# The last A12 x B21 products as seven products of halves, with sums made by accumulating transfers

## The chip, the core and the metric

The kernel runs on one core of a Trainium2 chip. The metric is device time of one execution in microseconds; the figure given for the kernel before is a median of three runs. The core's engines are TensorE (PE, matrix products; PEld is its weight load), VectorE (DVE), ScalarE (ACT), GpSimd (POOL) and SyncE (SP). SP issues most loads, POOL most stores and every transfer that adds into its destination. PSUM is where products are summed, here as four pairs of banks of 128 x 2 x 512 fp32; SBUF holds everything else that is worked on; DRAM holds inputs, outputs and scratch.

## What is computed

With x of 2048 tokens by 512, the output is a gated mix of a Fourier mixing and a SwiGLU layer:

```python
g = sigmoid((x * gate_w).sum(-1))
a = x @ dft_hid_re.T;  b = x @ dft_hid_im.T
y = dft_seq_re @ a - dft_seq_im @ b
h = silu(x @ w1) * (x @ w3)
out = g * y + (1 - g) * (h @ w2)
```

The hidden width F is 1376, padded to eleven chunks of 128. All of it is fp32.

## The kernel before, in words

**Three matmuls per product.** Every fp32 operand is split into a high part (fp32r, a rounded copy made by ScalarE) and a low part (the rest, by VectorE); `split` does it in lines 62 to 64. `mm3` (lines 69 to 72) then issues three matmuls for a pair of operands: high by high, high by low, low by high.

**Seven products instead of eight.** Each large product is cut in two halves in every direction, and the Strassen-Winograd scheme makes seven products of the halves. They are named P1 to P7. P1 = A11 x B11, P5, P6, P3, P7 and P4 use sums of blocks, and P2 = A12 x B21. P1, P6, P7 and P4 are summed one after another in one pair of PSUM banks, P5 and P3 in a second, P2 in a third. After each product the state of its banks is taken out where the scheme needs it.

**Stages.** The first stage makes a and b (scratch `ab`). The second makes the SwiGLU hidden values (scratch `hsp`); between its products, hooks call `work`, which takes the tasks of the list `later` one by one: these form the A-side operands of the last stage by `forms` (line 327) and store them, split, in the scratch `fsp`. The last stage is what the change touches. It has six *blocks*, (m, j): m = 0 is h @ w2, m = 1 the real part, m = 2 the imaginary part; j is the group of 1024 tokens. Blocks 4 and 5 are m = 2 with j = 0 and 1. In a block of m = 1 or 2 the A side is 512 output features by 2048 tokens to be summed over, the B side 2048 by 1024 tokens out (from the input `cc`).

**Steps.** A product of a block runs as four steps q of the list `STEPS` (lines 382 to 390), in the order of `CHAIN`: P1, P5, P6, P3, P7, P2, P4. A step of blocks 1 to 5 at full width is 12 matmuls of 512 columns. `step` (line 562) issues the matmuls of a step, then calls `advance`, then the tasks booked for that step in `TASKS`, and after a product's last step takes out the banks and calls `finish`, which makes the output of that quarter (for m = 2 with loaded tiles of the earlier blocks, `load_other`) and stores it.

**What runs ahead.** `advance(n)` does three things for later steps: `load_c(n + 8)` loads raw B blocks (B11, B12, B22, B21; a list sorted by the step that needs them less a small lead), `sum_c(n + 4)` makes the sums F1 = B11 + B12, F2 = F1 + B22, F3 = B12 + B22 and F4 = F2 + B21 in place by VectorE, and `split_c(n + 3)` splits the step's B operand. `BY_DMA` (line 413) names block 2: there F3 is made by a transfer of GpSimd that adds B12 from DRAM into the tile of B22, after B22's split (line 455).

**Buffers.** The pool f4 has 19 buffers of 128 x 1024 fp32 and holds raw B tiles, gates, sums taken from PSUM and tiles for outputs. zo has 8 (the split B operands of four steps). op has 28 and holds the split A operands: 7 products x 4 steps, loaded by `load_a` from `fsp`. The tile framework places the semaphore waits and picks buffers; it may also put an engine's instructions in another order than they are written, except that the loads issued through `fetch` keep theirs.

**The end.** The split sources of the last two steps (P4 of block 5) are multiplied by the gate first (lines 449 to 451), and these two steps write fresh banks in two row halves, so that the last output goes out in small pieces.

Of the kernel before, what the change touches and what calls it, by code (L numbers as in the profile page):

```python
# [7 lines left out]
F32 = mybir.dt.float32  # L8
# [4 lines left out]
P = 128  # L13
# [11 lines left out]
def fnet_swiglu_gate_kernel(  # L25
# [54 lines left out]
    ysp = dram.tile([G, 2, 2, P, 1024], F32, tag="ysp", name="ysp")  # L80
    PRODS = ("P1", "P5", "P6", "P3", "P7", "P2", "P4")
    wlsp = dram.tile([P, 1024], F32, tag="wlsp", name="wlsp")
    fsp = dram.tile([3, len(PRODS), NQ, P, 1024], F32, tag="fsp", name="fsp")


# [241 lines left out]
    def forms(m, q, ks, keep):  # L327
# [37 lines left out]

        return [load] + [lambda k=k: one(k) for k in ks]

    def fetch(o, i):
        tc.keep_in_program_order(nc.sync.dma_start(o, i))
# [9 lines left out]
    CHAIN = (("P1", "B11"), ("P5", "F1"), ("P6", "F2"), ("P3", "B22"),  # L379
             ("P7", "F3"), ("P2", "B21"), ("P4", "F4"))  # L380
    PLAIN = {"P3": "n1", "P7": "n1", "P2": "n0", "P4": "n01"}
    STEPS, AT = [], {}
    for b, (m, j) in enumerate(BLOCKS):
        for k, form in CHAIN:
            for q in range(NQS[m]):
                AT[b, k, q] = len(STEPS)
                STEPS.append((b, k, q, form))
            if m == 0 and k in PLAIN:
                STEPS.append((b, k, "pl", PLAIN[k]))
    NEED = (("B11", "P1", 0), ("B12", "P5", 1), ("B22", "P6", 1), ("B21", "P2", 0))  # L390
    LOADS = sorted((AT[b, k, q] - e, b, blk, q) for b, (m, j) in enumerate(BLOCKS)
                   for blk, k, e in NEED for q in range(NQS[m]))
    LEAD, AHEAD = 3, 5
    RAW, ZO, PL = {}, {}, {}

    def block(b, k, q):
        m, j = BLOCKS[b]
        if m == 0:
            v = hsp[j, int(k[1]) - 1, int(k[2]) - 1, 2 * q : min(2 * q + 2, NP)]
            return v.rearrange("c p n -> p c n")  # L400
        return half(cc[m - 1, j, ("B11", "B12", "B22", "B21").index(k), q])

    def chunks(b, q):
        return width(BLOCKS[b][0], q) // 256

    def load_c(n):
        while LOADS and LOADS[0][0] <= n:
            _, b, k, q = LOADS.pop(0)
            w = chunks(b, q)
            r = RAW[b, k, q] = raw(f"{k}_{b}_{q}", w * 512)  # L410
            fetch(half(r, w), block(b, k, q))

    BY_DMA = (2,)

    def sum_c(n):
        if not 0 <= n < len(STEPS):
            return
        b, k, q, form = STEPS[n]
        o = {"F1": "B12", "F2": "B22", "F4": "B21", "F3": "B22"}.get(form)
        if not o or q == "pl" or form == "F3" and b in BY_DMA:  # L420
            return
        t = RAW[b, "B12" if form == "F3" else "B11", q]
        nc.vector.tensor_add(t, t, RAW[b, o, q])  # L423

    def split_c(n):
        if not 0 <= n < len(STEPS):
            return
        b, k, q, form = STEPS[n]
        if q == "pl":
            r = PL[b]  # L430
            if form == "n1" and k == "P3":
                t = zo.tile([P, 1024], F32R, tag="zo", name=f"zp{n}")
                split(t[:, :512], t[:, 512:], r["n1"])
                r["z"] = t
            elif form == "n1":
                ZO[n] = r["z"][:, :512], r["z"][:, 512:]
                return
# [8 lines left out]
        f3 = "B22" if b in BY_DMA else "B12"  # L446
        src = RAW[b, {"F1": "B11", "F2": "B11", "F4": "B11", "F3": f3}.get(form, form), q]
        h, l = (zo.tile([P, w], F32R, tag="zo", name=f"z{v}{n}") for v in "hl")
        if n >= len(STEPS) - 2:

            nc.vector.tensor_mul(half(src), half(src), twice(GT[b], 0))
        split(h, l, src)
        ZO[n] = h, l
        if form == "B22" and b in BY_DMA:
            nc.gpsimd.dma_start(half(src, chunks(b, q)), block(b, "B12", q), accum_op=ALU.add)

    def advance(n):
        load_c(n + LEAD + AHEAD)
# [44 lines left out]
    def twice(t, n):  # L503
        return half(t)[:, n : n + 1].to_broadcast([P, 2, 512])
# [54 lines left out]
    U, BANKS, WHOLE = {}, {}, {}  # L559
    QUARTER = {"P3": (0, 1), "P7": (1, 1), "P2": (0, 0), "P4": (1, 0)}  # L560

    def step(n):
        b, k, q, form = STEPS[n]
        m, j = BLOCKS[b]
        end = b == len(BLOCKS) - 1
# [12 lines left out]
        fin = STEPS[n + 1][1] != k if n + 1 < len(STEPS) else True  # L578
# [24 lines left out]
        advance(n)  # L603
        for f in TASKS.pop(n, ()):
            f()
        if n == len(STEPS) - 3:
            U[k, b] = half(raw(f"u{k}_{b}"))
            finish(b, *QUARTER[k], U[k, b], whole)
        if not fin or n == len(STEPS) - 1:
            return  # L610
        if k in ("P1", "P5", "P6"):
            t = U[k, b] = half(raw(f"u{k}_{b}"))
            nc.scalar.activation(flat(t), flat(whole), AF.Copy)
# [51 lines left out]
    later += prep_w2l()  # L665
    for q in range(NQ):
        later += forms(2, q, PRODS, False)
    for q in range(NQ):
        later += forms(1, q, ("P1", "P5", "P6", "P3"), False)
    per = -(-len(later) // ((NC - 1) * 5))  # L670
# [122 lines left out]
```

## Time and profile before

| | us |
|---|---|
| median of 3 runs (708.13 to 708.25) | 708.18 |
| the profiled execution, as timed | 709.88 |
| its span in the profile | 708.1 |
| PE busy in the span | 702.6 |
| VectorE busy | 565.5 |
| ScalarE busy | 337.7 |
| GpSimd busy | 80.1 |

How to read the lines that follow. A group of instructions shows line, engine, operation, the tile written, an arrow and the tiles read, shapes and count, then busy us and mean ns of one, then the engine's idle time ahead of them and what ended it. A line of waits names who waited for whom, with the sum in us, the number of waits and the longest. A line of the timeline has start, length and instruction. A line of windows has the stretch, its length, then busy us and instruction count for PE, PEld, VectorE, ScalarE and GpSimd, and last the granted clock of TensorE, the busy share of the DMA engines and GB/s. A line of transfers has the issuing queue, the count, the size and the us from issue to landing. Because helpers record the splits, sums and loads, one source line stands for many tiles.

### The profile page before, as it was taken

The numbers are of one execution on the slowest core, as the hardware profiler recorded it, in microseconds if no ns is written. First come the engines' busy times: TensorE is split into PE (matmuls) and PEld (weight loads), VectorE is DVE, ScalarE is ACT, GpSimd is POOL, SyncE is SP. The second block draws the span as 40 slices with busy tenths as digits, with TensorE's granted clock in tenths as the row PEclk, the third lists the DMA queues.
The fourth block names the chain that finished last, engine by engine and source line by source line (L and its number), as shares of the span: only waits on it lengthen the run. The fifth ranks groups of instructions, "written<-read, shape, count | busy, mean of one in ns | idle before, by whom it ended". The sixth has DMA issues, their size and how long they took to land.

```text
span 708.1 us, 8582 instructions
## 1 busy us (share of the span) xinstructions
PE 702.6 (99%) x3081; PEld 578.9 (82%) x3081; DVE 565.5 (80%) x600; ACT 337.7 (48%) x380; POOL 80.1 (11%) x139
## 2 busy tenths in 40 slices
PE   9999999999999999999999999999999999999997
PEld 6888888888888888888888888888888888888886
DVE  6994358878988886859968997679488977999695
ACT  5744146655555454464453375444443444344431
POOL 0010103322323221100000001000000000000000
PEclk9999999999999999999999999999999999999999
DMA  8356439989999899889978869916889928971402
GB/s 302 116 190 224 179 118 343 310 302 323 377 370 390 303 356 377 295 331 402 342 271 299 287 251 261 319 41 238 303 313 341 371 98 279 336 244 64 149 31 89
DMA packets 55530, 186.43 MB, mean 263 GB/s; under 512 B 6012, under 2 KB 6268, under 8 KB 55488
## 3 DMA queue, kind: packets, MB, share of 16 engines
q1 hardware_dynamic: 36432, 117.59, 47.1%
q0 software_dynamic: 18768, 67.91, 25.5%
q8 instruction: 24, 0.39, 0.2%
q10 hardware_dynamic: 288, 0.39, 0.2%
q14 instruction: 18, 0.15, 0.1%
HBM read 119.54 MB, written 66.33 MB: 262 GB/s over the span
## 4 chain that ended last, share of the span: by engine, by line
PE 99%; DMA 1%; ACT 0%; DVE 0%; DVEq 0%; issue 0%
PE P L71 57%; PE X L71 17%; PE dP L71 10%; PE Z L71 8%; PE Y L71 4%; PE last L71 1%; PE dP L185 1%; DMA dB<-dd 1%; ACT dB21h L63 0%; DVE uP L556 0%; DVEq L789 0%
## 5 line engine op out<-in xcount | busy, mean ns | idle before, releaser
L63 ACT ACTIVATE zh<-B 128x1024 fp32r<-128x1024 f32 x154 | 157.2, 1023 | 216.9 <-PE P L71 192.5
L64 DVE TENSOR_TENSOR zl<-B,zh 128x1024 fp32r<-128x1024 f32 x154 | 180.0, 1173 | 58.6 <-ACT zh L63 53.1
L71 PE MATMUL P<-zh,a2P 128*128 128x512 f32 x432 | 133.1, 389 | 0.0
L423 DVE TENSOR_TENSOR B<-B,B 128x1024 f32<-128x1024 f32 (+1 forms) x84 | 97.1, 1168 | 0.4
L71 PEld LDWEIGHTS P<-zh,a2P 128*128 128x128 f32 x432 | 81.1, 188 | 16.9
L71 PE MATMUL P<-zh,a0P 128*128 128x512 f32 x280 | 87.5, 389 | 0.0
L71 PE MATMUL P<-zl,a2P 128*128 128x512 f32 x216 | 84.0, 389 | 0.0
L71 PE MATMUL P<-zh,a1P 128*128 128x512 f32 x256 | 79.1, 389 | 0.0
L71 PEld LDWEIGHTS P<-zh,a0P 128*128 128x128 f32 x280 | 52.5, 188 | 10.9
L71 PE MATMUL P<-zh,f1P 128*128 128x512 f32 x192 | 59.4, 389 | 0.0
L71 PEld LDWEIGHTS P<-zh,a1P 128*128 128x128 f32 x256 | 48.0, 188 | 9.9
L71 PE MATMUL P<-zl,a0P 128*128 128x512 f32 x140 | 54.5, 389 | 0.0
L71 PE MATMUL P<-zl,a1P 128*128 128x512 f32 x128 | 49.8, 389 | 0.0
L71 PEld LDWEIGHTS P<-zl,a2P 128*128 128x128 f32 x216 | 40.5, 188 | 8.4
L71 PEld LDWEIGHTS P<-zh,f1P 128*128 128x128 f32 x192 | 36.0, 188 | 7.5
L71 PE MATMUL P<-zl,f1P 128*128 128x512 f32 x96 | 37.3, 389 | 0.0
L71 PEld LDWEIGHTS P<-zl,a0P 128*128 128x128 f32 x140 | 26.3, 188 | 5.5
L71 PEld LDWEIGHTS P<-zl,a1P 128*128 128x128 f32 x128 | 24.0, 188 | 5.0
L618 DVE TENSOR_TENSOR uP<-uP,P 128x1024 f32<-128x1024 f32 x18 | 21.9, 1218 | 3.8 <-PE P L71 3.8
L271 DVE TENSOR_TENSOR s<-s,Y 128x1024 f32<-128x1024 f32 x11 | 13.4, 1215 | 11.6 <-PE Y L71 9.7
L293 DVE TENSOR_TENSOR u<-u,X 128x1024 f32<-128x1024 f32 x11 | 13.4, 1218 | 10.5 <-PE X L71 10.4
L71 PEld LDWEIGHTS P<-zl,f1P 128*128 128x128 f32 x96 | 18.0, 188 | 3.8
(1258 smaller groups left out, 1312.5 us busy)
## 6 DMA issues: line engine op xcount, KB each, us to landing
B<-cc SPq DMA_DIRECT2D x64, 512.0 KB, 5.3
fsp<-f2P POOLq DMA_DIRECT2D x28, 512.0 KB, 5.7
a2P<-fsp SPq DMA_DIRECT2D x28, 512.0 KB, 5.3
r<-ab SPq DMA_DIRECT2D x24, 512.0 KB, 5.8
hsp<-u POOLq DMA_DIRECT2D x20, 512.0 KB, 6.4
fsp<-f1P POOLq DMA_DIRECT2D x16, 512.0 KB, 6.5
B<-hsp SPq DMA_DIRECT2D x16, 512.0 KB, 10.1
a1P<-fsp SPq DMA_DIRECT2D x16, 512.0 KB, 6.8
```

Of the source, the lines that this page charges most:

```text
L63: nc.scalar.activation(hi, src, AF.Copy)
L64: nc.vector.tensor_sub(lo, src, hi.bitcast(F32))
L71: nc.tensor.matmul(ps, u, v, start=first and n == 0, stop=last and n == 2, skip_group_check=chain)
L185: nc.tensor.matmul(ps[i // 2][:, i % 2], u[:, 0, i * P : (i + 1) * P], v[:, 0], start=n == 0, stop=False, skip_group_check=True)
L271: nc.vector.tensor_add(S1[c], S1[c], flat(y))
L293: nc.vector.tensor_add(u4, u4, flat(x))
L423: nc.vector.tensor_add(t, t, RAW[b, o, q])
L618: nc.vector.tensor_add(flat(t), flat(t), flat(whole))
```

## The change

In blocks 4 and 5 the product P2 is no longer run per block. Since A12 of the imaginary part is the same for both token groups, A12 x [B21 of group 0, B21 of group 1] is one product of 256 x 1024 by 1024 x 1024, and it is cut in halves once more: seven inner products of 128 x 512 by 512 x 512, named LP1 to LP7. Each is two half steps of 6 matmuls; the 14 half steps are put between the steps of blocks 4 and 5 (`inner_step`), two of them after P6 of each block and the others mostly after every second step.

- *Order.* The two blocks run P1, P5, P6, P7, P3, P4 (`LORDER`), so P7 is now ahead of P3.
- *A side.* `inner_forms` loads A12 again in block 2, makes the inner sums, splits them and stores them in the scratch `lsp`; `load_inner` loads each eight steps ahead of its use. The four P2 operands of m = 2 are not formed in the second stage any more (`later[-2]`).
- *B side.* The inner blocks LB11, LB12, LB21, LB22 are the halves of B21 of both groups (two tiles each). Their sums LF1, LF2 and LF4 are made in the tile of LB11 by accumulating transfers after each split, LF3 in the tile of LB12.
- *F4 and F3.* F4 of blocks 4 and 5 is made by accumulating B21 into the tile of F2 after its split, in place of a load of B21 and a VectorE sum. F3 of block 5 is made in a fresh tile: B12 is loaded again and B22 accumulated. F3 of block 4 stays on VectorE.
- *Outputs.* `inner` takes each inner product from a PSUM bank of the fourth pair: two as negated copies by ScalarE, five as half-size additions or subtractions by VectorE, into the tile of P1's sum of block 4 or 5. The quarter (0, 0) of block 4 is finished after LP4, in block 5, that of block 5 after LP3. P1's bank of block 5 is added to a tile that is there already, by VectorE, where ScalarE copied it.
- *The gate* is multiplied into B11 of the last two steps as tasks at P3 of block 5.

```diff
+    def inner_forms():
+        st = {}
...
+        def load():
+            for h in range(2):
+                st[h] = raw(f"rl{h}")
+                for q in range(2):
+                    nc.sync.dma_start(
+                        st[h][:, q * 512 : (q + 1) * 512], ab[1, 1, 2 * h + q, :, 0].rearrange("p i e -> p (i e)"))
+
+        def one(k):
...
+            t = f4.tile([P, 2, 512], F32R, tag="f4", name=f"fl{k}")
+            split(quads(t[:, 0]), quads(t[:, 1]), src)
+            nc.gpsimd.dma_start(lsp[PRODS.index(k)], flat(t.bitcast(F32)))
+
+        return [load] + [lambda k=k: one(k) for k in ("P1", "P5", "P6", "P3", "P7", "P2", "P4")]
+
+    def load_inner(k):
+        t = A["L", k] = op.tile([P, 2, 4, P], F32R, tag="op", name=f"al{k}")
+        fetch(t.bitcast(F32).rearrange("p v c e -> p (v c e)"), lsp[PRODS.index(k)])
...
+    LB = (4, 5)
+    FORM = dict(CHAIN)
+    INNER = [(k, h) for k in ("P1", "P2", "P5", "P6", "P7", "P4", "P3") for h in range(2)]
...
+    LORDER = ("P1", "P5", "P6", "P7", "P3", "P4")
     for b, (m, j) in enumerate(BLOCKS):
-        for k, form in CHAIN:
+        for k, form in ((k, FORM[k]) for k in LORDER) if b in LB else CHAIN:
             for q in range(NQS[m]):
                 AT[b, k, q] = len(STEPS)
                 STEPS.append((b, k, q, form))
+                if b in LB and q % 2 and (b, k) not in ((LB[0], "P1"), (LB[0], "P5"), (LB[0], "P6"), (LB[1], "P6")):
+                    if len(todo) > 2:
+                        inner_step()
+            if b in LB and k == "P6":
+
+                for _ in range(2):
+                    inner_step()
...
     LOADS = sorted((AT[b, k, q] - e, b, blk, q) for b, (m, j) in enumerate(BLOCKS)
-                   for blk, k, e in NEED for q in range(NQS[m]))
+                   for blk, k, e in NEED if not (b in LB and blk == "B21") for q in range(NQS[m]))
+    LOADS += [(AT["L", k, h] - e, LB[1], "L" + blk, h) for blk, k, e in
+              (("B11", "P1", 0), ("B12", "P7", 4), ("B21", "P2", 0), ("B22", "P3", 3)) for h in range(2)]
+    LOADS += [(AT[LB[1], "P7", q] - 3, LB[1], "F3", q) for q in range(NQ)]
+    LOADS.sort()
...
             fetch(half(r, w), block(b, k, q))
+            if k in ("LB12", "F3"):
+                add_block(r, b, {"LB12": "LB22", "F3": "B22"}[k], q)
+
+    def add_block(t, b, k, q):
+        nc.gpsimd.dma_start(half(t, chunks(b, q)), block(b, k, q), accum_op=ALU.add)
...
-        if not o or q == "pl" or form == "F3" and b in BY_DMA:
+        if not o or q == "pl" or form == "F3" and b in BY_DMA + LB[1:] or form == "F4" and b in LB:
             return
...
-        if n >= len(STEPS) - 2:
-
-            nc.vector.tensor_mul(half(src), half(src), twice(GT[b], 0))
         split(h, l, src)
         ZO[n] = h, l
         if form == "B22" and b in BY_DMA:
-            nc.gpsimd.dma_start(half(src, chunks(b, q)), block(b, "B12", q), accum_op=ALU.add)
+            add_block(src, b, "B12", q)
+        elif form == "F2" and b in LB:
+            add_block(src, b, "B21", q)
+        elif form in ("LB11", "LF1", "LF2"):
+            add_block(src, b, {"LB11": "LB12", "LF1": "LB22", "LF2": "LB21"}[form], q)
...
+    INTO = {"P1": (0, 0), "P5": (1, 1), "P6": (0, 1), "P2": (0, 0), "P7": (1, 1), "P4": (1, 0), "P3": (0, 1)}
+    LPS = {}
+
+    def inner(n):
+        b, k, h, form = STEPS[n]
+        k = k[1:]
+        if h == 0:
+            if not LPS:
+                z = pair(3, "Lx")
+                LPS.update(P1=z[:, 0], P5=z[:, 1], P2=z[:, 1])
+        ps = LPS[{"P6": "P1", "P7": "P1", "P4": "P1", "P3": "P5"}.get(k, k)]
+        w = A["L", k]
+        zh, zl = ZO.pop(n)
+        for i in range(2):
+            c = slice(i * 512, (i + 1) * 512)
+            mm3(ps, w[:, 0, 2 * h + i], w[:, 1, 2 * h + i], zh[:, c], zl[:, c],
+                k in ("P1", "P5", "P2") and h == 0 and i == 0, h == 1 and i == 1, True)
+        advance(n)
+        for f in TASKS.pop(n, ()):
+            f()
+        if h == 1:
+            r, g = INTO[k]
+            if k == "P5":
+                U["P1", LB[1]] = half(raw("uL"))
+            t = U["P1", LB[g]]
+            if k in ("P5", "P6"):
+                nc.scalar.activation(t[:, r], ps, AF.Copy, scale=-1.0)
+            else:
+                (nc.vector.tensor_sub if g else nc.vector.tensor_add)(t[:, r], t[:, r], ps)
+            if k in ("P4", "P3"):
+                finish(LB[g], 0, 0, t)
...
-        if k in ("P1", "P5", "P6"):
+        if (k, b) in U:
+            nc.vector.tensor_add(flat(U[k, b]), flat(U[k, b]), flat(whole))
+        elif k in ("P1", "P5", "P6"):
...
         later += forms(2, q, PRODS, False)
+        later[-2] = lambda: None
...
-    for i, (k, q) in enumerate((k, q) for k, _ in CHAIN for q in range(NQ)):
+    for i, (k, q) in enumerate((k, q) for k in LORDER for q in range(NQ)):
         TASKS.setdefault(AT[3, "P1", 0] + 1 + 7 * i // 4, []).append(lambda k=k, q=q: load_a(2, k, q))
+    for i, f in enumerate(inner_forms()):
+        TASKS.setdefault(AT[2, "P1", 0] + 13 + 2 * i, []).append(f)
+    for k, h in INNER:
+        if not h:
+            TASKS.setdefault(AT["L", k, 0] - 8, []).append(lambda k=k: load_inner(k))
+    def gated(q):
+
+        t = half(RAW[LB[1], "B11", q])
+        tc.keep_in_program_order(nc.vector.tensor_mul(t, t, twice(GT[LB[1]], 0)))
+
+    for q in (2, 3):
+        TASKS.setdefault(AT[LB[1], "P3", q - 2], []).append(lambda q=q: gated(q))
```

More of the change, by code (lines that the diff above doesn't have):

```diff
@@ L82, in fnet_swiglu_gate_kernel @@
     wlsp = dram.tile([P, 1024], F32, tag="wlsp", name="wlsp")
+    lsp = dram.tile([len(PRODS), P, 1024], F32, tag="lsp", name="lsp")
     fsp = dram.tile([3, len(PRODS), NQ, P, 1024], F32, tag="fsp", name="fsp")
@@ L366, in forms, with cols, quads @@
         return [load] + [lambda k=k: one(k) for k in ks]
+    def inner_forms():
+        st = {}
+        def cols(t, v):
+            return t.rearrange("p (c h e) -> p c h e", c=4, h=2)[:, :, v]
+        def quads(ap):
+            return ap.rearrange("p (c e) -> p c e", c=4)
+        def load():
[5 more added lines that the diff above has]
+        def one(k):
+            a11, a21, a12, a22 = cols(st[0], 0), cols(st[0], 1), cols(st[1], 0), cols(st[1], 1)
+            if k in ("P5", "P3"):
+                st["m"] = raw(f"ml{k}")
+            lo, hi = quads(st["m"][:, :512]) if "m" in st else None, quads(st["m"][:, 512:]) if "m" in st else None
+            if k == "P5":
+                src = st["s5"] = lo
+                nc.vector.tensor_sub(src, a22, a21)
+            elif k == "P6":
+                src = st["s6"] = hi
+                minus_sum(src, st["s5"], a11)
+            elif k == "P3":
+                src = lo
+                minus_sum(src, a12, st["s6"])
+            elif k == "P7":
+                src = hi
+                nc.vector.tensor_sub(src, a11, a21)
+            else:
+                src = {"P1": a11, "P2": a12, "P4": a22}[k]
+            t = f4.tile([P, 2, 512], F32R, tag="f4", name=f"fl{k}")
[5 more added lines that the diff above has]
+        fetch(t.bitcast(F32).rearrange("p v c e -> p (v c e)"), lsp[PRODS.index(k)])
     def fetch(o, i):
@@ L387, in fnet_swiglu_gate_kernel @@
                 STEPS.append((b, k, q, form))
+                if b in LB and q % 2 and (b, k) not in ((LB[0], "P1"), (LB[0], "P5"), (LB[0], "P6"), (LB[1], "P6")):
[4 more added lines that the diff above has]
+                    inner_step()
             if m == 0 and k in PLAIN:
                 STEPS.append((b, k, "pl", PLAIN[k]))
+    assert not todo
+    FINAL = {}
+    for n, (b, k, q, form) in enumerate(STEPS):
+        FINAL[b, k] = n
     NEED = (("B11", "P1", 0), ("B12", "P5", 1), ("B22", "P6", 1), ("B21", "P2", 0))
     LOADS = sorted((AT[b, k, q] - e, b, blk, q) for b, (m, j) in enumerate(BLOCKS)
[L392 removed]
+                   for blk, k, e in NEED if not (b in LB and blk == "B21") for q in range(NQS[m]))
[3 more added lines that the diff above has]
+    LOADS.sort()
     LEAD, AHEAD = 3, 5
@@ L397, in block @@
         m, j = BLOCKS[b]
+        if k[0] == "L":
+            return half(cc[m - 1, int(k[3]) - 1, 3, 2 * (int(k[2]) - 1) + q])
         if m == 0:
@@ L400, in block @@
             return v.rearrange("c p n -> p c n")
-        return half(cc[m - 1, j, ("B11", "B12", "B22", "B21").index(k), q])
+        return half(cc[m - 1, j, ("B11", "B12", "B22", "B21").index("B12" if k == "F3" else k), q])
     def chunks(b, q):
@@ L445, in split_c @@
         w = chunks(b, q) * 512
-        f3 = "B22" if b in BY_DMA else "B12"
-        src = RAW[b, {"F1": "B11", "F2": "B11", "F4": "B11", "F3": f3}.get(form, form), q]
+        f3 = "B22" if b in BY_DMA else "F3" if b == LB[1] else "B12"
+        inner = form[0] == "L"
+        blk = form[1:] if inner else form
+        src = RAW[b, "L" * inner + {"F1": "B11", "F2": "B11", "F4": "B11", "F3": "B12" if inner else f3}.get(blk, blk), q]
         h, l = (zo.tile([P, w], F32R, tag="zo", name=f"z{v}{n}") for v in "hl")
-        if n >= len(STEPS) - 2:
-            nc.vector.tensor_mul(half(src), half(src), twice(GT[b], 0))
         split(h, l, src)
@@ L564, in step @@
         m, j = BLOCKS[b]
+        if k[0] == "L":
+            if q == 0 and k in ("LP4", "LP3"):
+                load_other(LB[k == "LP3"], 0, 0)
+            return inner(n)
         end = b == len(BLOCKS) - 1
@@ L577, in step @@
         own = k in ("P1", "P5", "P2")
-        fin = STEPS[n + 1][1] != k if n + 1 < len(STEPS) else True
+        fin = n == FINAL[b, k]
         zh, zl = ZO.pop(n)
```

7 lines of the change are left out of this document (added).

## The prediction

> **What bounds the kernel now.** I read the page's engine shares first, then the chain of waits in order of time, then the windows of the last four blocks (76.2 us each, counted back from the end of the last product).
>
> ```profile
> span 708.1 us, 8582 instructions
> PE 702.6 (99%) x3081; PEld 578.9 (82%) x3081; DVE 565.5 (80%) x600; ACT 337.7 (48%) x380; POOL 80.1 (11%) x139
> ...
> 293.61 405.28 PE P L71 x1788
> 698.89 5.45 PE last L71 x24
> ...
> 399.60:475.80 76.20, 76.20 (x338) 63.10 (x337) 62.95 (x62) 37.46 (x43) 5.66 (x8) 1.00 0.69 226
> 552.00:628.20 76.20, 76.20 (x338) 63.10 (x337) 65.88 (x58) 32.53 (x32) 2.71 (x4) 1.00 0.75 269
> 628.20:704.40 76.20, 76.13 (x336) 62.69 (x334) 64.90 (x58) 29.09 (x28) 2.87 (x4) 1.00 0.30 102
> ```
>
> TensorE (PE) is the bound without a gap: the chain is matmul from 293.61 to 704.34, 405.28/1788 = 0.2267 us each, at granted clock 1.00. A step of 12 is 2.72 us, a half step of 6 is 1.36 us. So matmuls that go are time won, as long as nothing else makes PE wait. In the windows the last two columns are the share of the DMA engines and GB/s: VectorE (DVE) is at 86% in block 4 (552 to 628), the transfers at 0.75 there and 0.30 in block 5.
>
> What feeds PE is a split three steps ahead (ScalarE copy, VectorE subtract), and what feeds the split is a tile out of the 19 buffers of f4:
>
> ```profile
> ACT zh L63 <- PE P L71: 192.5, 126, 3.0
> ...
> SPq L369 <- DVE zl L64: 94.9, 38, 15.2
> ...
> L64 DVE TENSOR_TENSOR zl<-B,zh 128x1024 fp32r<-128x1024 f32 x140 | 170.7, 1221 | 54.9 <-ACT zh L63 49.9 <-PE P L71 4.4
> L63 ACT ACTIVATE zh<-B 128x1024 fp32r<-128x1024 f32 x140 | 148.4, 1062 | 193.3 <-PE P L71 174.6 <-DMA B<-cc 7.0 <-ACT uP L613 4.5
> ...
> L64 DVE TENSOR_TENSOR zl<-B,zh 128x512 fp32r<-128x512 f32 x14 | 9.6, 688 | 3.6 <-ACT zh L63 3.2
> ```
>
> ScalarE waits for PE (the eight zo buffers hold four steps), so the split for step n+3 starts when step n-1 ends; it takes 1.06 + 1.22 = 2.3 us of the 8.16 us that three whole steps give. The load queue (SP) waits for splits to free f4 buffers, so a load is as early as a free buffer lets it be.
>
> **The change part by part.** *Removed:* 8 steps of 12 matmuls (96); *added:* 14 half steps of 6 (84). 12 x 0.2267 = **2.72 us less** on the path.
>
> *VectorE.* Block 4 has 58 operations now, about 1.135 us apart (65.88/58). After: 32 splits, 12 sums (F1, F2, F3), 2 bank additions, 6 operations of the outputs of P7 and P3, 2 left from block 3 = 54, and two of half size (0.69): 54 x 1.135 + 1.4 = 62.7 of 76.2 us. Block 5: 30 splits, 8 sums, the new addition of P1's bank, 2 of P7 and P3, 3 of block 4's P4, 5 of LP4 and LP3, 4 of P7 and P3, 2 gatings = 55, 3 halves: 64.5 of 73.4 us. Covered on the whole. The shorter steps cost lead: two whole and a half give 6.8 us, less 2.3 = 4.5 us of slack; around the two half steps after P6 5.44 - 2.3 = 3.1 us. In P1 and P5 of block 5 there are 28 operations (31.8 us) in 27.2 us, 4.6 us behind, about the slack. I take 0, bound 0 to 2 us; P6 behind it has little on VectorE and catches up.
>
> *The A side.* Four forms and seven splits of 512 elements on VectorE (11 x 0.69 = 7.6 us), seven copies on ScalarE, in blocks 2 and 3; block 2's VectorE is at 62.95 of 76.2 us, so covered; without cover it would cost those 7.6 us. Four splits in the first stage fall away. Taking P1's bank by VectorE in place of ScalarE, the gatings moved three steps ahead, P3 behind P7, and the inner evictions into two banks of the free pair (each has over 5 us before the bank is written again) cost nothing while VectorE keeps the slack above.
>
> *The transfers* are what matters. Twenty accumulating ones come in: F4 of blocks 4 and 5 (8), LB11, LF1 and LF2 (6), LF3 (2), F3 of block 5 (4). Four such run now, in block 2. The rows are GpSimd's issues, ScalarE's splits that wait for them, then the windows:
>
> ```profile
> 426.78 0.92 POOL L455 DMA_DIRECT2D B<-cc  x1 [24.25 <-DVE zl L64]
> 429.71 0.88 POOL L455 DMA_DIRECT2D B<-cc  x1 [2.01 <-DVE zl L64]
> 432.66 0.84 POOL L455 DMA_DIRECT2D B<-cc  x1 [2.07 <-DVE zl L64]
> 435.79 0.83 POOL L455 DMA_DIRECT2D B<-cc  x1 [2.29 <-issue]
> ...
> 435.59 1.06 ACT L63 ACTIVATE zh<-B 128x1024 fp32r<-128x1024 f32 x1 [1.42 <-DMA B<-cc]
> 439.49 1.07 ACT L63 ACTIVATE zh<-B 128x1024 fp32r<-128x1024 f32 x1 [2.83 <-DMA B<-cc]
> 443.31 1.06 ACT L63 ACTIVATE zh<-B 128x1024 fp32r<-128x1024 f32 x1 [2.76 <-PE P L71]
> 447.13 2.96 ACT L63 ACTIVATE zh<-B 128x1024 fp32r<-128x1024 f32 x3 [2.76 <-DMA B<-cc]
> ...
> 432.00:446.00 14.00, 14.00 (x64) 11.58 (x63) 8.91 (x9) 5.17 (x5) 1.68 (x2) 1.00 1.05 281
> 446.00:448.00 2.00, 2.00 (x10) 1.69 (x9) 1.90 (x2) 0.87 (x1) 0.00 (x0) 1.00 0.99 393
> ...
> B<-cc SPq DMA_DIRECT2D x64, 512.0 KB, 5.3
> B<-cc POOLq DMA_DIRECT2D x4, 512.0 KB, 10.1
> ```
>
> Issued 3.0 us apart, they land (447.13 - 435.59)/3 = 3.85 us apart, with the engines full (1.05). In 3.85 us at 281 GB/s 1.08 MB move: one accumulating transfer (0.524 MB) and one plain load. A plain one at 393 GB/s is 1.33 us, so an accumulating one is **2.5 us** of all 16 engines. Bounds: 1.33 (if it costs what a load does) and 3.85 (if the load beside it was free). The splits ran 3.85 us apart where PE takes 2.72: four of them ate 3 to 4 us of lead, and it held.
>
> The Trainium skill (DMA: Bandwidth & Descriptors, section "Anatomy of one DMA — SWDGE (gpsimd) path") fits a transfer of GpSimd as 2.0 us plus bytes over 436 GB/s, with no extra for an accumulating one. By it 0.524 MB move in an estimated 1.2 us, the twenty in 24 us, and there would be no stall in the sum below: 705.5 us. The trace's 3.85 us for a pair speaks against it.
>
> The budget runs from the first to the last of them that PE needs. The first: P6 q0 of block 4 is split when step 4 ends, 552.0 + 5 x 2.72 + 2.3 = 567.9. The last: P7 q3 of block 5 has 15 whole and 6 half steps ahead in its block, so it starts at 628.2 + 49.0 = 677.2 and its split must start by 674.9. 107 us, less 0.9 of issue and the fixed part of a landing (3.1 - 1.33 = 1.8): 104 us.
>
> ```profile
> 568.00:675.00 107.00, 107.00 (x474) 88.60 (x473) 90.27 (x79) 46.78 (x45) 2.90 (x4) 1.00 0.56 192
> ...
> a2P<-fsp SPq DMA_DIRECT2D x5, 512.0 KB, 4.7
> ...
> DMA to landing us min/median/max: 3.1/5.3/13.0
> ...
> 634.65 23.20 SPq L369 DMA_DIRECT2D B<-cc  x4
> ```
>
> Now 192 GB/s x 107 us = 20.5 MB move in it, at 393 GB/s 52.3 us. Twenty at 2.52 add 50.4. Plain loads: four of F3, about six more of the A side (seven and P4's four where five of a2P are issued there now), two fewer of B21 (LB11 comes ahead): 8 x 1.33 = 10.7. Sum 113.4 us in 104: 9.4 us too much; 5.4 if the last two loads of "o" and a store may go behind. I take **7 us**. (At 1.33: 89.6, no stall. At 3.85: 140, 36 us late, far off, since four in a row with loads were not that slow.)
>
> It falls on P7 of block 5, because there the buffers run out too. Held in P5: B11 4, B22 4, LB22 2, gates 2, sums for P1 2, "o" of LP4 2, the bank of P5 1, and one of LF2 until LP4's split: 18 of 19, and four F3 are asked for. The last F3 load waits until LP4's output frees its "o" (655.4 + 0.69 + 1.2, about 657.5); after it come its landing (5.3), the issue and an accumulation behind those of F4 (10.1 in a row of four, here eight): 673.8 at best, against 674.9. That this queue of loads stands still for buffers is seen now too: four loads take 23.20 us. What is late next: ScalarE takes splits in order, so those of P3 wait behind P7's; what they read is there by then. On GpSimd's queue an accumulation that waits for its load (F3, LB12) holds up the F4 ones and the stores of outputs behind it: P4 waits for the former, with eight steps to spare, and nothing before the end for the latter, except that their buffers come free later.
>
> **Sum.** The profiled execution took 709.88 us, its span of 708.1 and 1.8 around it: 709.88 - 2.72 + 7 = 714.2. The median of the runs shown, 708.18, is 1.70 below it, so as a median **712.5 us**. The rivals' times are medians too.
>
> **Rivals.** *The transfers stay hidden* (705.5). GpSimd's queue may take F3's accumulations ahead of F4's, which P4 needs only 22 us after P7 begins (eight steps): with the four of F4 (10 us) out of the way the sum is 103.4 in 104. Below 2.0 us for one, or with F3 first, it decides. For it: share 0.30 in block 5, and PE rode out block 2. Against: 12 of the 20 come in block 4 already, and F3's loads get buffers last.
>
> *A heavier overload* (720). At 2.9 us for one the sum is 121.4: up to 17.4 late, 15 in the middle, 708.2 - 2.7 + 15 = 720.5. Then block 4 stalls too: LB11 to LF1 to LF2 are two accumulations in series, LP5's split to LP6's 13.6 us apart, against 10.1 us landing, plus 2.3 and 0.9. For it: share 1.05 in block 2 while they ran.
>
> *VectorE decides.* The 4.6 us lag in P1 and P5 of block 5 passes the 4.5 us slack, with the sums issued in another order, by 1 to 2 us: 707 us, the transfers being hidden.
>
> **How the numbers follow.** Forecast 0.43, hidden 0.33, heavier 0.16, VectorE 0.08. About 1.4 us (0.2%) is what a measurement can tell from none. Faster 0.33, same 0.08, slower 0.59. The range takes in the hidden case and most of the heavier: 705.2 to 720; the forecast's own is 709.6 to 716.
>
> **What would show it.** Right: 3069 matmuls, DMA share near 1 from 580 to 675, and PE's only gaps ahead of P7 of block 5, released by splits that wait for the DMA on F3; about 3.85 us or more between landings of accumulating transfers. Hidden: no gap on PE, span 2.7 us shorter. Heavier: gaps ahead of LP5, LP6 or LP7 too. VectorE: gaps whose split waited for no DMA. A slower first stage or block 2 would mean that the A side was not covered.

## The result, and the profile after

The changed kernel takes **717.35 us** (median of 5 runs, 713.89 to 719.72) against 708.18 before in the same series: ratio 1.0124, 95% interval 1.0093 to 1.0155, so it is slower. The profiled execution is the quickest of the five, 713.89 us. A second series with the same kernel gave 716.35 (714.35 to 717.38), ratio 1.0104 (1.0082 to 1.0127).

The page of after, its first lines (span, then busy us, share and instructions of each engine):

```profile
span 712.1 us, 8671 instructions
PE 700.6 (98%) x3069; PEld 576.7 (81%) x3069; DVE 564.1 (79%) x605; ACT 344.4 (48%) x390; POOL 98.8 (14%) x162
```

The twelve matmuls are gone (3081 to 3069), and PE, which had no gap from 300 us on, now has one. Its waits there, and the matmuls at the place:

```profile
PE P L71 <- ACT zh L63: 5.2, 1, 5.2
PE P L71 <- DVE zl L64: 0.5, 1, 0.5
```

```profile
675.29 0.39 PE L71 MATMUL P<-zh,a2P 128*128 128x512 f32 x1
680.91 0.80 PE L71 MATMUL P<-zh,a2P 128*128 128x512 f32 x1 [5.23 <-ACT zh L63]
```

It is one gap, ahead of the last quarter of P7 of block 5. The first matmul behind it takes 0.80 instead of 0.39 us. The windows of 2 us (PE busy in the third column, the granted clock third from the end, then the share of the DMA engines and GB/s) say why:

```profile
674.00:676.00 2.00, 1.68 (x8) 1.06 (x6) 0.00 (x0) 0.00 (x0) 0.00 (x0) 1.00 1.05 270
676.00:678.00 2.00, 0.00 (x0) 0.00 (x0) 0.00 (x0) 0.00 (x0) 0.00 (x0) 1.00 1.08 283
678.00:680.00 2.00, 0.00 (x0) 0.00 (x0) 0.00 (x0) 0.19 (x1) 0.00 (x0) 0.55 0.76 281
680.00:682.00 2.00, 0.80 (x1) 0.29 (x1) 1.10 (x1) 2.00 (x3) 0.00 (x0) 0.50 0.15 20
...
684.00:686.00 2.00, 2.00 (x8) 1.58 (x7) 2.00 (x3) 0.00 (x0) 0.04 (x1) 0.74 0.00 0
```

PE stands from 675.7 to 680.9 (by its pace of one matmul in 0.2267 us the next was due at 675.5). Until the split starts at 679.8 no engine computes, and the DMA engines are full (1.05 and 1.08). The granted clock goes from 1.00 to 0.50 within the window from 678 (its mean of 0.55 puts the step near 678.2, 2.5 us into the gap) and comes back within that from 684 (0.74: near 685.0, 4.1 us after the first matmul). Now the chain of waits, in order of time, and GpSimd's issues of the accumulations for F3 (tile F) and F4 (tile B):

```profile
659.57 7.47 DMA F<-cc
667.07 2.16 issue
669.25 10.46 DMA F<-cc
679.81 1.06 ACT zh L63
...
702.63 5.45 PE last L71 x24
```

```profile
648.00 0.88 POOL L493 DMA_DIRECT2D F<-cc  x1 [12.33 <-DMA F<-cc]
652.54 0.84 POOL L493 DMA_DIRECT2D B<-cc  x1 [3.66 <-DVE zl L64]
653.17 1.11 POOL L493 DMA_DIRECT2D F<-cc  x1
655.46 0.85 POOL L493 DMA_DIRECT2D B<-cc  x1 [1.18 <-issue]
659.25 0.84 POOL L493 DMA_DIRECT2D F<-cc  x1 [2.94 <-issue]
662.30 0.86 POOL L493 DMA_DIRECT2D B<-cc  x1 [2.21 <-DVE uP L594]
665.40 0.85 POOL L493 DMA_DIRECT2D B<-cc  x1 [2.23 <-DVE zl L64]
669.25 0.84 POOL L493 DMA_DIRECT2D F<-cc  x1 [3.00 <-issue]
```

The last F3 load is issued at 659.57 and lands 7.47 us later; the accumulation is issued last of all, behind the four of F4, at 669.25, and takes 10.46 us. The split starts at 679.81.

What lets that load go at 659.57 is VectorE. The tile `o` that it takes over comes free with the second of two additions to the output of LP4. Here are LP4's last matmul and these additions:

```profile
653.53 0.39 PE L71 MATMUL Lx<-zh,alP 128*128 128x512 f32 x1
```

```profile
656.59 0.68 DVE L676 TENSOR_TENSOR uP<-uP,Lx 128x512 f32<-128x512 f32 x1
...
658.32 1.22 DVE L628 TENSOR_TENSOR uP<-o,uP 128x1024 f32<-128x1024 f32 x1
```

VectorE takes LP4's bank 2.7 us after the product is done. It is busy only 3.89 of 8 us from 620 to 628, waiting for tiles that land late (7.01 of 8 in the run without the additions below), and then without a pause from 628 to 660.

The account of this execution: the last run of products starts at 291.75, 1.86 us earlier than before. With the 405.28 + 5.45 us of before less 2.72, its last matmul would end at 699.76; it ends at 702.63 + 5.45 = 708.08. The 8.3 us lost are 5.4 us of gap, 0.5 us for the low part of the split, 2.2 us put down to the half clock (108 matmuls are left at 680.91: 24.5 us at 0.2267 and the 0.5 us, while 27.2 pass) and 0.2 us ahead of the gap.

Two windows for comparison with before: the whole stretch of the budget, and block 2, where the A side's work went.

```profile
568.00:675.00 107.00, 106.91 (x472) 88.26 (x471) 83.02 (x75) 49.49 (x49) 19.58 (x24) 1.00 1.01 294
```

```profile
399.60:475.80 76.20, 76.20 (x338) 63.16 (x337) 67.60 (x73) 42.92 (x51) 9.37 (x15) 1.00 0.84 283
```

The engines' share went from 0.56 to 1.01 over 107 us, VectorE's busy time fell from 90.27 to 83.02. In block 2 VectorE does 4.65 us more, and PE stays at 76.20 of 76.20.

### The profile page after: what moved, and what is told of

Read it like the earlier page. It is cut to its first block, busy times and chain, and to the rows that moved or that the text cites. A ratio compares the mean times of both kernels' runs of the same rounds, so it can differ in the third digit from the quotient of the medians.

```text
span 712.1 us, 8671 instructions
## 1 busy us (share of the span) xinstructions
PE 700.6 (98%) x3069; PEld 576.7 (81%) x3069; DVE 564.1 (79%) x605; ACT 344.4 (48%) x390; POOL 98.8 (14%) x162
## 4 chain that ended last, share of the span: by engine, by line
PE 89%; DMA 5%; DVE 3%; issue 1%; ACT 0%; DVEq 0%; POOLq 0%; ACTq 0%
PE P L71 48%; PE X L71 17%; PE dP L71 10%; PE Z L71 8%; PE Y L71 4%; DMA F<-cc 3%; DVE zl L64 2%; DMA B<-cc 1%; PE Lx L71 1%; DMA o<-nbsp 1%; PE last L71 1%; DMA dB<-dd 1%; DVE B L505 1%; DVE uP L628 1%; PE dP L186 0%
## 5 line engine op out<-in xcount | busy, mean ns | idle before, releaser
L63 ACT ACTIVATE zh<-B 128x1024 fp32r<-128x1024 f32 x142 | 143.9, 1018 | 171.4 <-PE P L71 140.7
L64 DVE TENSOR_TENSOR zl<-B,zh 128x1024 fp32r<-128x1024 f32 x142 | 165.1, 1169 | 40.3 <-ACT zh L63 34.8
L71 PE MATMUL P<-zh,a2P 128*128 128x512 f32 x368 | 117.0, 393 | 5.2 <-ACT zh L63 5.2
L71 PEld LDWEIGHTS P<-zh,a2P 128*128 128x128 f32 x368 | 69.9, 190 | 20.1 <-ACT zh L63 5.7
L505 DVE TENSOR_TENSOR B<-B,B 128x1024 f32<-128x1024 f32 (+1 forms) x72 | 82.7, 1161 | 2.1 <-DMA B<-cc 1.7
L71 PE MATMUL P<-zl,a2P 128*128 128x512 f32 x184 | 72.5, 394 | 0.6 <-DVE zl L64 0.5
L71 PEld LDWEIGHTS P<-zl,a2P 128*128 128x128 f32 x184 | 35.0, 190 | 8.7 <-DVE zl L64 1.5
L64 DVE TENSOR_TENSOR zl<-LB,zh 128x1024 fp32r<-128x1024 f32 x14 | 17.1, 1222 | 8.1 <-ACT zh L63 8.1
L63 ACT ACTIVATE zh<-LB 128x1024 fp32r<-128x1024 f32 x14 | 14.8, 1058 | 17.8 <-PE P L71 12.8
L294 DVE TENSOR_TENSOR u<-u,X 128x1024 f32<-128x1024 f32 x11 | 13.4, 1219 | 10.5 <-PE X L71 10.4
```

The costliest lines, as they stand in the source:

```text
L63: nc.scalar.activation(hi, src, AF.Copy)
L64: nc.vector.tensor_sub(lo, src, hi.bitcast(F32))
L71: nc.tensor.matmul(ps, u, v, start=first and n == 0, stop=last and n == 2, skip_group_check=chain)
L294: nc.vector.tensor_add(u4, u4, flat(x))
```

## The experiments

All edits are against the changed kernel, but for the first, which is a kernel by itself. "Before" beside each was between 707.88 and 708.12.

**The price by itself.** Stretches of 16 transfers each, with no computing:

```diff
+    for i in range(N):
+        keep(nc.gpsimd.dma_start(half(a[i]), src(i), accum_op=ALU.add))
+    barrier(a)
...
```

> This kernel computes nothing of the reference: it only moves tiles of 128 x 1024 fp32 (512 KB), in four stretches apart from each other: 16 plain loads by SP, 16 plain loads by GpSimd, 16 accumulating transfers by GpSimd, then 16 accumulating ones by GpSimd beside 16 plain loads by SP. If adding is what costs (about 2.5 us of all 16 engines where a load takes 1.33), the stretches take about 21, 21, 40 and 62 us, each with a share of the engines near 1. If an accumulating transfer costs what a load does and the loss in the kernel came from the order of the queues, the third takes 21 and the fourth 43 us. If GpSimd's issue is the limit, 3.0 us for each whatever it does, the second and the third both take about 48 us, with the engines' share well below 1 in both.

Its windows (only VectorE and GpSimd have columns here, then clock, share, GB/s):

```profile
4.00:26.00 22.00, 1.32 (x16) 0.00 (x0) 1.00 1.01 397
26.00:62.00 36.00, 0.00 (x0) 8.63 (x16) 1.00 1.03 410
70.00:106.00 36.00, 0.00 (x0) 10.95 (x14) 1.00 1.06 202
116.00:152.00 36.00, 0.00 (x0) 11.94 (x14) 1.00 1.05 198
```

Nothing held back the plain loads of the fourth stretch: SP issued them from 15.46 us on, so they ran beside the end of the first stretch and the second, and the last two stretches are accumulations alone. Accumulations beside plain loads were thus not measured by themselves. All four rows have full engines. A plain tile of 0.524 MB takes 0.524/397 = 1.32 us from SP alone and 0.524/410 = 1.28 us from both queues, an accumulating one 0.524/202 = 2.60 and 0.524/198 = 2.65 us. Adding costs as much again as moving, and with the engines full neither GpSimd's issue nor the order of queues has a part in it. The fit of the Trainium skill (DMA: Bandwidth & Descriptors, section "Anatomy of one DMA — SWDGE (gpsimd) path") names 436 GB/s for any such transfer: the plain rows come near it, the accumulating ones are at less than half, and the rows decide.

**The change without the additions.** The twenty transfers stay on their queue, in their order, as copies; the sums that they made are left out.

```diff
-        nc.gpsimd.dma_start(half(t, chunks(b, q)), block(b, k, q), accum_op=ALU.add)
+        if b in LB:
+            nc.gpsimd.dma_start(half(t, chunks(b, q)), block(b, k, q))
...
```

> The twenty accumulating transfers of blocks 4 and 5 are plain copies of the same bytes from the same queue, at the same places, with the same waits (the sums they made are left out: each tile holds only the block copied last). Transfer theory with a price of 2.5 us for an accumulating and 1.33 for a plain transfer: 20 x 1.2 = 23 us of transfers go, no gap at P7, median 705.5 to 707.5. If the number of transfers, their waits or the buffers are the cause and not what adding costs: 713 to 719 as the changed kernel.

Measured 705.59 us (705.45 to 705.89), ratio 0.9965 (0.9952 to 0.9978). PE waits for nothing in the last two blocks. The budget's window:

```profile
568.00:675.00 107.00, 107.00 (x474) 88.63 (x473) 85.92 (x77) 52.83 (x53) 13.05 (x23) 1.00 0.86 310
```

The same bytes and more pass (310 against 294 GB/s) in a share of 0.86, and the whole gain of the twelve matmuls is there: 708.18 - 2.72 = 705.46. So the loss is the adding, and VectorE, the A side, the order of the products and the two half steps after P6 cost nothing while it is away. VectorE's lag goes with it: LP4's last matmul ends at 653.4 there and its bank is taken at 654.12, 0.7 us later instead of 2.7.

**Fewer accumulations: F3 of block 5 by VectorE**, from B12, which so is kept until P7 (no loads and no accumulations of F):

```diff
-    LOADS += [(AT[LB[1], "P7", q] - 3, LB[1], "F3", q) for q in range(NQ)]
...
-        f3 = "B22" if b in BY_DMA else "F3" if b == LB[1] else "B12"
+        f3 = "B22" if b in BY_DMA else "B12"
```

> F3 of block 5 is made by VectorE in the tile of B12, as in block 4; four accumulating transfers and four loads of B12 go. Transfer theory (the 16 DMA engines are over-full from block 4 on and the last F3 lands late): 4 x 2.5 + 4 x 1.33 = 15 us of transfers go, which is more than the wait of some 7 to 12 us; PE has no gap at P7 of block 5, median 705.5 to 707.5. VectorE theory (VectorE's lag sets the time): four more operations of 1.14 us in block 5, so not faster than the changed kernel, 717 to 722.

713.62 us (713.12 to 714.42), ratio 1.0079 (1.0064 to 1.0094): both theories missed. The wait at P7 is gone and another one is there; PE's waits, and SP's issues (start, length, tile):

```profile
PE Lx L71 <- DMA alP<-lsp: 4.7, 1, 4.7
```

```profile
661.82 0.33 SPq L416 DMA_DIRECT2D o<-nbsp  x1
662.24 0.43 SPq L416 DMA_DIRECT2D alP<-lsp  x1
```

The A operand of LP3 stands in SP's queue behind the second output tile of LP4, which gets a buffer at 661.82 only: the four B12 hold theirs until P7. From 640 to 660 the share of the engines is 0.60. What the transfers gave back, the 19 buffers took.

**The same with LP3's A operand loaded 16 steps ahead**, past those tiles in the queue:

```diff
-            TASKS.setdefault(AT["L", k, 0] - 8, []).append(lambda k=k: load_inner(k))
+            TASKS.setdefault(AT["L", k, 0] - (16 if k == "P3" else 8), []).append(lambda k=k: load_inner(k))
```

> As the first experiment (F3 of block 5 by VectorE, without its four loads and four accumulations), and LP3's A operand is loaded 16 steps ahead instead of 8, so that it stands ahead of LP4's two output tiles in SP's queue. If the 4.7 us wait of the first experiment came from the order of that queue (a load standing behind loads that wait for a buffer), it goes: 706 to 707.5 us, the transfers being no bound with 16 accumulating ones. If the buffers as such are short, another load waits in its place and the time stays at 711 to 714. If the transfers are still the bound, the waits at P7 come back with a share near 1 from 580 to 675: above 711.

710.35 us (709.69 to 712.64), ratio 1.0039 (1.0026 to 1.0053), between the first two cases expected. The operand is there in time, and the buffers make the next thing late. PE's waits in the last blocks, and the chain:

```profile
PE P L71 <- DVE zl L64: 3.5, 2, 2.9
```

```profile
661.20 7.53 DMA o<-nbsp
...
669.96 1.23 DVE zl L64
```

The output tile of LP4, issued at 661.20, now holds VectorE until it lands, and a split of P7 stands behind it there: PE waits 2.9 us. This profiled run is the slowest of the five. Its last matmul ends 7.1 us later than its start would give (at 706.79, where 291.72 and the 408.01 us of all products give 699.73); 3.5 us of that are waits, and most of the rest passes with the granted clock at 0.50, from 670.5 to 677.4.

**F4 of block 5 by VectorE**, with B21 loaded again and the gate multiplied at the split, as in the kernel before:

```diff
+    LOADS += [(AT[LB[1], "P4", q] - 1, LB[1], "B21", q) for q in range(NQ)]
...
-        elif form == "F2" and b in LB:
+        elif form == "F2" and b == LB[0]:
...
```

> F4 of block 5 is made by VectorE again from a loaded B21 (the gate stands at the split as before the change); four accumulating transfers become four plain loads. Transfer theory: 4 x (2.5 - 1.33) = 4.7 us of transfers go and no F4 stands ahead of F3 on GpSimd's queue; wait at P7 0 to 4 us, median 706 to 710. Buffer theory (F3 is late because f4 has no free buffer, not because the engines are full): B21 takes four buffers more, so no better than the changed kernel, 716 or more. VectorE theory: 4.6 us more work, 717 or more.

711.76 us (711.25 to 714.63), ratio 1.0066 (1.0044 to 1.0087). With four accumulations fewer, P7 has no wait over 0.2 us. VectorE is late at the end instead; two lines of the timeline, its gating and a matmul of the last quarter:

```profile
693.91 2.36 DVE L535 TENSOR_TENSOR B<-B,gate 128x1024 f32<-128x1024 f32 x2
```

```profile
697.54 0.47 PE L71 MATMUL last<-zh,a2P 128*128 128x512 f32 x1 [0.92 <-ACT zh L63]
```

From 670 to 700 PE is busy 28.15 of 30 us, with the engines' share at 0.51: there VectorE's work on F4 and the gate costs time, and the transfers no longer do.

**F4's accumulations behind F3's.** They are issued at LP3, all else stays:

```diff
-        elif form == "F2" and b in LB:
+        elif form == "F2" and b == LB[0]:
...
+    for q in range(NQ):
+        TASKS.setdefault(AT["L", "P3", q // 2], []).append(lambda q=q: late_f4(q))
```

> The four accumulations of F4 of block 5 are issued behind those of F3 on GpSimd's queue (at LP3); nothing else differs, the transfers are the same in number and kind. Transfer theory with the queue's order: 10 us of work no longer stand ahead of F3, the sum is 103 us in 104, median 706 to 710. If only the total counts, or the F3 loads' wait for buffers: 714 to 718.

708.63 us (706.07 to 714.66, 10 runs), ratio 1.0010 (0.9985 to 1.0035). In the profiled run nothing waits at P7. What is left lies earlier; one line of its chain and one of its windows:

```profile
620.08 10.00 DMA B<-cc
```

```profile
620.00:640.00 20.00, 18.31 (x80) 14.51 (x79) 13.41 (x13) 8.75 (x9) 2.40 (x3) 1.00 1.01 322
```

A load of B12 of block 5 gets its buffer at 620.08, when VectorE has made an output of block 4 and so let go of a tile, and lands 10 us later in full engines; PE is busy 18.31 of 20 us.

**Stores off GpSimd's queue.** Two runs: the stores alone, and the stores with F4 behind F3.

```diff
-            return nc.gpsimd.dma_start(rows, t)
+            return nc.scalar.dma_start(rows, t)
```

> The changed kernel with only the output stores of line 631 issued through ScalarE's queue; F4's accumulations of block 5 stay ahead of F3's. If the place of F4's accumulations is what makes P7 late, the wait at P7 stays with a share near 1 from 580 to 675: 712 to 717 us. If the late buffers alone made it (stores behind waiting accumulations), it goes: 706 to 708.

> As the fourth experiment (F4's accumulations of block 5 behind those of F3), and the outputs of full quarters are stored through ScalarE's queue instead of GpSimd's, where they stand behind accumulations that wait. If the wait left near 630 us (B12 of block 5 late because buffers of output tiles come free late) comes from that, the late store is gone and the time is 705.5 to 707.0. If it is the engines' load alone, it stays at 707.5 to 709 with the wait near 630. If ScalarE's splits now stand behind a store that waits for VectorE, PE gets new gaps released by ScalarE: above 710.

Alone: 716.86 us (716.08 to 718.16), ratio 1.0120 (1.0103 to 1.0137), no gain. PE's wait and the end of the chain are those of after:

```profile
PE P L71 <- ACT zh L63: 5.4, 1, 5.4
```

```profile
660.76 8.33 DMA F<-cc
...
671.50 10.03 DMA F<-cc
```

With F4 behind F3: 707.09 us (706.12 to 708.29, 10 runs), ratio 0.9988 (0.9978 to 0.9997), and in the profiled run PE waits for nothing in the last blocks. Counted from the start of the products (294.21 here, 291.75 in after), the last accumulation of F3 goes out 4.4 us sooner than in after (at 667.34) and its split starts 7.3 us sooner (at 674.99). So it is the place of F4's accumulations that makes P7 late. What the stores add to it isn't settled, since this interval and that of F4 behind F3 alone overlap; the runs spread over 2.2 us instead of 8.6.

**And one buffer more:** the gate of block 5 is loaded at P6 instead of P1.

```diff
-        act(b, "P1", lambda b=b: load_gate(b))
+        act(b, "P6" if b == LB[1] else "P1", lambda b=b: load_gate(b))
```

> F4's accumulations of block 5 behind F3's and the output stores through ScalarE's queue, as in the run before, and the gate of block 5 is loaded at P6 instead of P1, which frees one of the 19 buffers for that time. If what is left over 705.6 us (the time with the additions left out) is the shortage of buffers, this gives 705.5 to 706.8; if it is the engines' load, it stays at 706.5 to 707.5.

**706.03 us** (705.42 to 708.45, 12 runs), ratio 0.9963 (0.9951 to 0.9974): quicker than before and than the changed kernel, with all twenty accumulations in it. GpSimd's issues, and two windows:

```profile
660.78 0.85 POOL L493 DMA_DIRECT2D F<-cc  x1 [2.97 <-DVE uP L628]
661.41 1.10 POOL L871 DMA_DIRECT2D B<-cc  x1
...
672.22 0.84 POOL L871 DMA_DIRECT2D B<-cc  x1 [4.36 <-DVE zl L64]
```

```profile
568.00:675.00 107.00, 107.00 (x472) 88.30 (x472) 88.70 (x81) 52.88 (x53) 17.16 (x20) 1.00 1.00 291
...
675.00:690.00 15.00, 15.00 (x68) 12.44 (x67) 12.64 (x11) 5.32 (x5) 1.51 (x2) 1.00 0.80 241
```

The last accumulation of F3 goes out at 660.78, in after at 669.25. The engines are as full as there up to 675 (1.00), and what is late now is F4 (share 0.80 from 675 to 690), which nobody waits for. Whether the freed buffer is what brought the last microsecond isn't shown. The median is 1.06 us below that of the run without the later gate, and the interval lies below that one's (0.9978 to 0.9997). But the two were set against different runs of the kernel before, of which six of 17 here lie near 710 and none of 14 there. And the profiled run without the later gate loses nothing in the last blocks: it took 708.29 because its products start at 294.21, 2.59 us later than without the additions (291.62). Only one run of each series has a trace, so how the others started isn't known.

**More room for descriptors, and the changed kernel again.** GpSimd's waits of up to 3 us with no semaphore ("issue" in the rows of after) could come from room that is short.

```diff
-    nc = bacc.Bacc("TRN2", target_bir_lowering=False, num_devices=1, dynamic_dma_scratch_size=1024)
+    nc = bacc.Bacc("TRN2", target_bir_lowering=False, num_devices=1, dynamic_dma_scratch_size=2048)
```

> The changed kernel with room for twice as many descriptors of GpSimd's transfers (2048 instead of 1024), and nothing else. GpSimd's accumulations of F3 show waits of up to 3 us that no semaphore ends. If these come from that room and make P7's operands late, they go, and the time is 706 to 710. If the engines are simply full (share near 1 from 580 to 675), issuing earlier changes nothing: 713 to 719 with the same wait at P7.

> The changed kernel once more, on the chip of the two runs that follow. It gave 713.9 to 719.7 us, the version with twice the descriptor room 713.9 to 715.0. If that room matters, this comes out at 716 to 719 again; if the difference is only the scatter of runs whose transfers are the bound, it is at 714 to 716, and the wait at P7 is there in any case.

With twice the room: 714.39 us (713.91 to 714.98), ratio 1.0091 (1.0076 to 1.0106). Its chain:

```profile
659.74 9.45 DMA F<-cc
...
669.22 0.54 issue
...
669.77 9.85 DMA F<-cc
```

The issue wait falls from 2.16 to 0.54 us, the load ahead of it takes 9.45 instead of 7.47: PE still waits 5.0 us at P7. The time only changes its name, which fits full engines. The interval overlaps that of the second series of the changed kernel, so whether the room is worth a microsecond stays open; it is not the cause. The profiled run of that second series (716.80 us) differs from the first by 2.9 us. Here are the first twelve matmuls in its chain (start, length), then in that of the first series:

```profile
6.14 4.64 PE dP L186 x12
```

```profile
5.72 3.01 PE dP L186 x12
```

They end at 10.78 and at 8.73: the second series' run is 2.05 us later here, and 0.9 of the 2.9 us are lost from there on. The execution of before that the prediction was counted from is of the late sort: its chain goes on behind those twelve at 10.59.

## Why the prediction came out as it did

- *Twelve matmuls less, 2.72 us:* right. Without the additions the kernel takes 705.59, where the sum says 705.46.
- *VectorE and the A side at nothing:* right for PE's own path. PE has no wait in the run without additions, and it has no gap in block 2. The two half steps after P6 with their smaller slack cost nothing either. The rival in which VectorE decides did not come. But VectorE was not free: with the additions it took LP4's bank 2.7 us late, and so let the buffer of the last F3 go late. The prediction counted no lag there.
- *2.5 us for one accumulating transfer,* read off a pair in block 2 as 3.85 less a plain one: right within 6%, though from one place with loads beside it. By itself it is 2.60 to 2.65, a plain one 1.28 (taken: 1.33); the pair would be 3.88. Both bounds, and the rule without an extra for adding, are out.
- *The budget of 113.4 us in 104, 5.4 to 9.4 late:* right in kind. In the 107 us of the window 294 GB/s moved 31.5 MB. Counted as twenty accumulations (10.5 MB, 52 us at 2.62) and 21.0 MB of loads and stores at some 400 GB/s (393 in block 2, 397 to 410 by themselves; 52 us), that is 104 to 105 us, and the engines' share is 1.01.
- *P7 of block 5, by the last F3 load:* right, with its quarter. The steps were forecast as 657.5, landing 5.3, issue 0.9 and 10.1, so 673.8; they are 659.57, 7.47, 2.2 and 10.46, so 679.7. The forecast's times are those of an execution whose products start at 293.61, and this one's start 1.86 us earlier. On the forecast's clock it is 661.4 and 681.6: 7.8 us later, of which the load's buffer is 3.9, its landing 2.2, the issue 1.3 and the accumulation 0.4. The second series, which starts at 293.82, gives 7.8 as well. So the chain as written (673.8 against the 674.9 by which the split was due) would have given no stall; the 7 us came from the budget alone. The buffer is late because VectorE is, and the landing was taken from the median over the whole kernel (5.3), and in full engines it isn't that.
- *7 us of stall:* the term that was too small. The two profiled runs lose 8.3 and 9.2 (in the second the products start at 293.82, so would end at 701.83, and end at 710.98). Of the first, 5.9 is waiting, near the lower end of 5.4 to 9.4; the 2.2 us of half clock behind the gap were in no step of the prediction. The split is 6.8 us late, but PE starts with the high part 1.1 us behind the split's start, where the prediction gave it the whole 2.3. The gap bought the half clock, and so cost more than itself. The waiting was taken too long and the clock not at all; the two errors partly cancel, so that 7 lies nearer to 8.3 by some luck.
- *The step from the profiled execution to the median, 1.70 less:* did not carry over. It took for granted that the changed kernel's median lies as far below a run that starts like the profiled one of before. The second series' profiled run starts so (10.78 us against 10.59 for the end of the first twelve matmuls) and took 716.80, where 714.2 was forecast; the first series' starts early and took 713.89, 1.4 above 712.5. But the medians are 717.35 and 716.35, and how the executions at the median started isn't known. So 712.5 was 4.85 too low: as a sum that is 2.6 against such a run, mostly the stall's size, 1.7 by this step, and 0.55 by which the median lies above that run.
- *The rival with F3 ahead of F4* was a rival of order, and its mechanism is right: 103.4 us in 104. GpSimd's order of after is F, B, F, B, F, B, B, F, with F3's last accumulation behind all of F4's, so it did not happen by itself; written so, it takes the wait at P7 away, and with the stores and the gate moved the time is 706.03. The forecast itself had F3's last accumulation behind those of F4; as a rival the prediction left the other order to a chance of 0.33 with the words that the queue "may take" F3 first; following when each accumulation's tile is ready (F4's right after the splits of P6, F3's only after late loads) would have given the order.
- *The heavier overload:* not seen. Block 4 loses nothing, LP5, LP6 and LP7 do not wait. (By the prediction's own terms its sum at 2.9 us is 121.0, not 121.4.)

## What to carry to other kernels

A sum made by an accumulating transfer is paid with the DMA engines: 2.6 us of all 16 for 512 KB, twice a plain load, so count it in the transfers' budget over the stretch in which its result is due, as VectorE's 1.22 us are counted in VectorE's. When the engines are full, order decides, as it did here by some 8 to 10 us: what is wanted first has to be issued first on the queue, and what has eight steps to spare goes behind. A relief that keeps tiles longer moves the wait to whatever is loaded into the buffers next; look there before counting it as a gain.

## What was not expected of the hardware

The gap is dearer than its length: 2.5 us after the last matmul the granted clock goes to 0.50, and matmuls follow one another every 0.43 us instead of 0.23 until it is back 4.1 us after the next: 2.2 us in all. Neither time is fixed. In the second series of the changed kernel the clock falls 4.3 us into the gap and is back 5.9 us after the next matmul. With F3 by VectorE and the early A operand a wait of 2.9 us was enough: the clock falls 2.2 us into it and is back 6.1 us after the next matmul. Here is the window of the fall in the second series, then in that run (the clock is third from the end):

```profile
682.00:684.00 2.00, 0.80 (x1) 0.29 (x1) 1.04 (x1) 2.00 (x3) 0.00 (x0) 0.52 0.04 14
```

```profile
670.00:672.00 2.00, 0.77 (x2) 0.68 (x3) 2.00 (x3) 0.00 (x0) 0.75 (x1) 0.63 0.44 104
```

The Trainium skill (TensorE: Matmul & The Clock Gate, section 'Part 1: The HAM clock gate (the "warmup" mystery)') states half clock after an idle window of some 3.4 us, and full clock again after as long a busy one. The three runs agree in kind, but not in the figure: the fall came after 2.2 to 4.3 us and the return after 4.1 to 6.1 us.

The scatter is not explained. Without the additions five runs lie within 0.44 us; with F4 behind F3 ten runs spread over 8.6 us (706.07 to 714.66), of one and the same program. The load alone does not set it: with the stores moved too, ten runs spread over 2.2 us, and the engines' share from 568 to 675 is 0.99 in that profiled run and 0.98 in the other. And twelve matmuls at the start took 3.01 us in one run and 4.64 in another of the same kernel, with the granted clock shown as 1.00 in both, which nothing in the change touches.
